# Masking every attention unit in one VectorE step instead of by way of GpSimd, with two small scalars of the first tiles moved to ScalarE

## The chip, the cores and the metric

The kernel runs on one core of one Trainium2 chip. The metric is the device time of one execution in microseconds, taken as the median of several executions. A profile is of one execution; its span is the time between the first and the last recorded instruction.

## The reference

Three layers follow one another on 1152 tokens (2 batches of 576) of width 512:

```python
# attention: B, H, S, D = 2, 8, 576, 64, all f32
scores = scale * np.matmul(q, k.transpose(0, 1, 3, 2))
kth = np.partition(scores, -32, axis=-1)[..., -32:-31]
scores = np.where(scores >= kth, scores, -1e9)
attn = np.exp(scores - scores.max(-1, keepdims=True))
attn = attn / (attn.sum(-1, keepdims=True) + 1e-9)
x = attn @ v                      # heads side by side: 1152 x 512
# mixture of 8 experts, all experts on all tokens, gates by 8 Sinkhorn rounds
for e in range(8):
    out += P[:, e:e+1] * (np.maximum(x @ w1[e], 0) @ w2[e])   # 512 -> 1024 -> 512
# a last feed-forward layer, 512 -> 2048 -> 512, with Mish between the products
```

So each row of attention keeps only the scores that reach its 32nd largest one.

## The kernel before, in words

The 1152 tokens are 9 tiles of 128 rows. A unit of attention is one tile t and one head h, 72 units in all, in the order of t and then h. Each unit passes five stages: `scores` (TensorE products, copied by ScalarE to a tile `s` of 128x576), `threshold` (VectorE takes the largest 8 values four times with `max`, and strikes them out three times with `match_replace`, which gives the 32 largest, `top`), `mask`, `norm` and `values` (TensorE turns the probabilities, multiplies by v, and the result becomes `xh` and `xl`, two float32r parts of x).

The first 13 units (`POOL_UNITS`) are "pooled". Their `mask` has three steps: VectorE writes 0 or a very negative number to `em` (L285), GpSimd adds the scores to it (L286), and ScalarE takes the exponential in place and sums it while it does so (L272, with VectorE writing the bias `nb`, the negated and scaled maximum, on L271). The other units take the exponential of all the scores to a tile `e` already in `threshold`, and `mask` is a single VectorE instruction, which compares, multiplies and sums (L290). In `norm`, VectorE adds epsilon to the sum (L299) and takes the reciprocal (L300), and ScalarE scales the unit's row (L305). Pooled units take `norm` and `values` one step later than the others.

Tiles 0 and 1 are the first chunk. Once their x is there, the experts' feed-forward passes of chunk 0 begin on TensorE (`h_c0e` on L619, `y_c0e` on L596), then those of chunk 1, with the rest of attention woven in between at a fixed rate; after attention, chunk 2 (`c2e`) and the last layer (`d`) follow. The first `max` of each unit of tile 2 is ordered on VectorE behind the last reciprocal of tile 1 (`live["ends"]`).

The order on TensorE is written out by hand: the plan runs step by step, and step i holds the scores of unit i, then the later stages of earlier units, then `early` scores of later tiles, which are kept in buffers of theirs or sent to memory. The orders on the other engines come from a planner, which takes the ready instruction of the highest priority: stream "first" is ahead of "evict", "prep" (weights, L517 to L522, with GpSimd computing the low parts `wl`), "attn" and "moe". Within a stream the order of the program counts. GpSimd also computes the low parts of k (`ks`, L158) and q (L188).

Rotating buffers: `top`, `nb`, `sm` and `r` have 4 each, `s` 6, `w` and `e` 2, and `em` 3 pairs.

Of the kernel before, what the change touches and what calls it, by code (L numbers as in the profile page):

```python
# [10 lines left out]
F32 = mybir.dt.float32  # L11
F32R = mybir.dt.float32r
U32 = mybir.dt.uint32
AF = mybir.ActivationFunctionType
ALU = mybir.AluOpType
# [4 lines left out]
P = 128  # L20
B, H, S, D = 2, 8, 576, 64
# [13 lines left out]
TOPK = 32  # L35
NEG = -3.0e38
SCALE = 0.125
EPS = 1e-9
TINY2 = ((1 + 1 / 16) * 2.0**-15) ** 2

CHUNKS = [(0, 1), (2, 3), (4, 5, 6, 7, 8)]
# [2 lines left out]
LAG = 2  # L44
LAG2 = 2
AHEAD = 2
POOL_UNITS = 13
EARLY = [(t, h) for t in (2, 3) for h in range(H)] + [(t, h) for t in (5, 6) for h in range(HG)]
EARLY_FROM, EARLY_PER_STEP = 5, 2
HOLD, RATE = 8, 0.25  # L50
# [23 lines left out]
def attention_moe_moe2(ctx: ExitStack, tc: tile.TileContext, qT, kT, vm, vt, wg, wst, w64, out):  # L74
    nc = tc.nc
    st = Streams(
        tc, {"first": 0, "evict": 200_000, "prep": 500_000, "attn": 1_000_000, "moe": 2_000_000, "fill": 3_000_000}
    )
    ctx.enter_context(tc.manual_schedule(engines={mybir.EngineType.PE}))

    def after(inst, earlier):

        tc.add_manual_dep(
            inst.ins,
            earlier.ins.name,
            mybir.DependencyInfo(mybir.DependencyClass.NoSync, mybir.DependencyReason.DATA),
            reason="order",
        )

    def pool(name, bufs=1, space=None, stack=ctx, side="left", **kw):  # L90
        if space is not None:
            kw["space"] = space
        return stack.enter_context(tc.tile_pool(name=name, bufs=bufs, side=side, **kw))

    const = pool("const")
    small = pool("small", 4)
# [13 lines left out]
    sp = pool("sp", 2, stack=att)  # L110
# [35 lines left out]
    qset, live, away = {}, {}, {}  # L146
# [45 lines left out]
    def queries(t, g):  # L192
        if (t, g) not in qset:
            qset[t, g] = load_q(t, g)
        return qset[t, g]
# [46 lines left out]
                load_v(t // 4, h // 2)  # L242
        yield

    def threshold(t, h, on_pool):

        with st("attn"):
            s = live["s", t, h]
            top = small.tile([P, TOPK], F32, tag="top", name=f"top_{t}_{h}")
            w = sp.tile([P, S], F32, tag="w", name=f"w_{t}_{h}")  # L250
            src = s
            for i in range(TOPK // 8):
                g = top[:, 8 * i : 8 * i + 8]
                top8 = nc.vector.max(g, src)  # L254
                if i == 0 and t == CHUNKS[0][-1] + 1:
                    if "ends" in live:
                        after(top8, live["ends"])
                    else:
                        live.setdefault("held", []).append(top8)
                if i + 1 < TOPK // 8:  # L260
                    nc.vector.match_replace(w, g, src, NEG)  # L261
                    src = w
            live["top", t, h] = top
            if not on_pool:
                live["e", t, h] = exponential(t, h, sp.tile([P, S], F32, tag="e", name=f"e_{t}_{h}"), s, nc.vector)
        yield from ()

    def exponential(t, h, dst, src, eng, **kw):

        nb = small.tile([P, 1], F32, tag="nb", name=f"nb_{t}_{h}")  # L270
        eng.tensor_scalar(nb, live["top", t, h][:, 0:1], -SCALE, None, op0=ALU.mult)  # L271
        nc.scalar.activation(dst, src, AF.Exp, bias=nb, scale=SCALE, **kw)  # L272
        return dst

    def mask(t, h, on_pool):

        with st("attn"):
            s = live.pop(("s", t, h))
            sm = small.tile([P, 1], F32, tag="sm", name=f"sm_{t}_{h}")
            kth = live["top", t, h][:, TOPK - 1 : TOPK]  # L280
            if h % 2 == 0:
                live["pair", t, h] = sp.tile([P, 2 * S], F32, tag="em", name=f"em_{t}_{h}", bufs=3)
            em = live["pair", t, h - h % 2][:, h % 2 * S :][:, :S]
            if on_pool:
                nc.vector.tensor_scalar(em, s, kth, NEG, op0=ALU.is_lt, op1=ALU.mult)  # L285
                nc.gpsimd.tensor_tensor(em, em, s, ALU.add)  # L286
                exponential(t, h, em, em, nc.vector, accum_out=sm)
            else:
                e = live.pop(("e", t, h))
                nc.vector.scalar_tensor_tensor(em, s, kth, e, op0=ALU.is_ge, op1=ALU.mult, accum_out=sm)  # L290
            live["em", t, h], live["sm", t, h] = em, sm
        yield from ()

    def norm(t, h, on_pool):
        with st("attn"):
            em, sm = live["em", t, h], live.pop(("sm", t, h))
            r = small.tile([P, 1], F32, tag="r", name=f"r_{t}_{h}")
            with st("moe" if on_pool else "attn"):
                nc.vector.tensor_scalar(r, sm, EPS, None, op0=ALU.add)  # L299
                inv = nc.vector.reciprocal(r, r)  # L300
            if (t, h) == (CHUNKS[0][-1], H - 1):
                live["ends"] = inv
                for inst in live.pop("held", ()):
                    after(inst, inv)
            nc.scalar.activation(em, em, AF.Copy, scale=r)  # L305
        yield from ()
# [96 lines left out]
    def attention():  # L403
        with st("attn"):
            load_k(0, 0)
            queries(0, 0)
            load_k(0, 1)
            wgraw = const.tile([P, NC, E], F32, name="wgraw")
            nc.sync.dma_start(wgraw, wg)
            nc.gpsimd.tensor_copy(wgs[:, :, :E], wgraw)  # L410
            nc.gpsimd.tensor_sub(wgs[:, :, E : 2 * E], wgraw, wgs[:, :, :E])
        units = [(t, h) for t in range(NT) for h in range(H)]
        plan = {}
        for u, (t, h) in enumerate(units):
            pooled = u < POOL_UNITS
            for order, (stage, delay) in enumerate(
                (
                    (scores, 0),
                    (partial(threshold, on_pool=pooled), AHEAD),
                    (partial(mask, on_pool=pooled), AHEAD + 1),  # L420
                    (partial(norm, on_pool=pooled), AHEAD + (2 if pooled else 1)),
                    (values, AHEAD + (3 if pooled else 2)),
                )
            ):
                plan.setdefault(u + delay, []).append((order, u, partial(stage, t, h)))
        stores = {}

        def early(t, h):

            k = EARLY.index((t, h))  # L430
            if k < 2:
                x = xfirst.tile([P, S], F32, tag=("xh1", "xl1")[k], name=f"early{k}")
            elif k < 10:
                name = ("xh2", "xl2")[(k - 2) // 4]
                if (k - 2) % 4 == 0:
                    stores[name] = xlast.tile([P, 4, S], F32, tag=name, name=f"early_{name}")
                x = stores[name][:, (k - 2) % 4, :]
            else:
                with st("attn"):
                    x = sp.tile([P, S], F32, tag="away", name=f"early{k}", bufs=2)  # L440
            yield from scores(t, h, x)
            if k >= 10:
                with st("attn"):
                    away[t, h] = dram.tile([P, S], F32, tag=f"away_{t}_{h}", name=f"away_{t}_{h}")
                    nc.sync.dma_start(away[t, h], live.pop(("s", t, h)))

        def fetch(t, h):
            with st("attn"):
                for b in range(t * P // S, (t * P + P - 1) // S + 1):
                    for i in range(h, h + HG):  # L450
                        if (b, i) not in ks:
                            load_k(b, i)
                queries(t, h // HG)
            yield from ()

        for k, (t, h) in enumerate(EARLY):
            step = EARLY_FROM + k // EARLY_PER_STEP
            plan[step].append((9, k, partial(early, t, h)))
            if h % HG == 0:
                plan[step - 2].append((8, k, partial(fetch, t, h)))  # L460
        for i in sorted(plan):
            runs = [run for _, _, run in sorted(plan[i], key=lambda x: x[:2])]
            blocks = 2 if i % 2 else 4
            for k, _ in enumerate(chain.from_iterable(run() for run in runs)):
                yield i + min(k + 1, blocks) / blocks
# [198 lines left out]


    at = attention()
    for _ in at:
        if live.get("done") == CHUNKS[0][-1]:
# [191 lines left out]
```

## Time and profile before

| | us |
|---|---|
| Time, median of 3 runs | 1221.68 (1221.15 to 1223.91) |
| Time of the profiled execution | 1221.39 |
| Span of the profile | 1219.6 |
| Busy PE / DVE / ACT / POOL in the span | 1168.7 / 854.7 / 660.2 / 540.8 |

PE is TensorE, PEld its weight loads, DVE is VectorE, ACT ScalarE, POOL GpSimd, SP the queue that issues most DMAs. Busy time counts the stretches in which an engine executes; a mean over the whole span hides that stages have different limits, so the stages have to be looked at one by one. Consecutive instructions of an engine overlap a little in the records, so what one costs its queue is the distance from its start to the next start.

### The profile page before, as it was taken

Reading aid. Unit: us, or ns where it says so; the run is one execution under the profiler, and the core shown is the slowest. Engines: PE = TensorE matmul, PEld = TensorE weight load, DVE = VectorE, ACT = ScalarE, POOL = GpSimd, SP = SyncE. Lnnn points to the kernel's source line nnn. Section 1 sums busy time; section 2 is a strip of 40 time slices with the busy share of each in tenths; the row PEclk is TensorE's granted clock in tenths of the full one; section 3 lists DMA queues with packets and bytes.
Section 4 is the critical chain, followed back from the end, with each engine's and each line's share of the span. In section 5 each row is a group of like instructions: output and inputs, shape, how many; then the busy total and the mean of one; then the engine's idle time right before and its main releaser. Section 6 shows DMA issues by size and latency. Waiting matters only on the chain.

```text
span 1219.6 us, 21194 instructions
## 1 busy us (share of the span) xinstructions
PE 1168.7 (96%) x7459; PEld 1048.4 (86%) x7459; DVE 854.7 (70%) x1873; ACT 660.2 (54%) x1321; POOL 540.8 (44%) x424
## 2 busy tenths in 40 slices
PE   2677999999999999999999999999999999999998
PEld 2566888998989899899999999999999999999997
DVE  7999999999999999713656868677666633433221
ACT  6786777877777778654223333333333334554432
POOL 7844778877777877774112112121121122221210
PEclk9899999999999999999999999999999999999999
DMA  8434565576655555665235665656445332223201
GB/s 258 126 129 152 171 178 170 170 224 188 211 163 168 157 162 164 186 220 169 70 89 180 199 190 176 207 178 192 138 134 160 119 98 64 93 95 114 78 26 44
DMA packets 105114, 183.20 MB, mean 150 GB/s; under 512 B 14128, under 2 KB 24624, under 8 KB 105008
## 3 DMA queue, kind: packets, MB, share of 16 engines
q1 hardware_dynamic: 103712, 180.68, 47.6%
q8 instruction: 58, 0.95, 0.3%
q10 hardware_dynamic: 1296, 1.18, 0.3%
q14 instruction: 48, 0.39, 0.1%
HBM read 158.55 MB, written 23.27 MB: 149 GB/s over the span
## 4 chain that ended last, share of the span: by engine, by line
PE 86%; DVE 11%; DMA 1%; ACT 1%; issue 0%; POOL 0%; SPq 0%; POOLq 0%; ACTq 0%
PE h_c2e L619 18%; PE y_c2e L596 18%; PE h_d L619 8%; PE y_d L596 8%; PE y_c0e L596 7%; PE h_c0e L619 7%; PE h_c1e L619 6%; PE y_c1e L596 6%; DVE top L254 4%; DVE w L261 4%; PE pv L348 2%; PE tr L325 2%; PE sc L226 2%; PE pv L355 1%; DVE em L290 1%; DMA wraw_c0e<-in_wst_dram 1%
## 5 line engine op out<-in xcount | busy, mean ns | idle before, releaser
L522 POOL TENSOR_TENSOR wl_c2e<-wraw_c2e,wh_c2e 128x512 fp32r<-128x512 f32 x64 | 84.2, 1315 | 341.2 <-ACT wh_c2e L520 326.5
L522 POOL TENSOR_TENSOR wl_c0e<-wraw_c0e,wh_c0e 128x512 fp32r<-128x512 f32 x128 | 171.6, 1356 | 53.1 <-ACT wh_c0e L520 50.9
L522 POOL TENSOR_TENSOR wl_c1e<-wraw_c1e,wh_c1e 128x512 fp32r<-128x512 f32 x128 | 173.3, 1371 | 48.6 <-ACT wh_c1e L520 45.2
L520 ACT ACTIVATE wh_c2e<-wraw_c2e 128x512 fp32r<-128x512 f32 x128 | 80.8, 632 | 186.9 <-PE y_c2e L596 95.0
L254 DVE MAX8 top<-w 128x8 f32<-128x576 f32 x216 | 157.8, 747 | 0.8
L619 PE MATMUL h_c2e<-xh,wh_c2e 128*128 128x256 f32 (+1 forms) x512 | 158.3, 309 | 0.0
L619 PE MATMUL h_c2e<-xl,wh_c2e 128*128 128x256 f32 (+1 forms) x512 | 158.0, 309 | 0.0
L619 PE MATMUL h_c2e<-xh,wl_c2e 128*128 128x256 f32 (+1 forms) x512 | 157.8, 308 | 0.0
L538 DVE SCALAR_TENSOR_TENSOR hl_c2e<-h_c2e,hh_c2e 128x256 fp32r<-128x256 f32 (+1 forms) x128 | 62.5, 488 | 99.7 <-ACT hh_c2e L537 99.3
L596 PE MATMUL y_c2e<-wh_c2e,hh_c2e 128*128 128x512 f32 x320 | 126.0, 394 | 0.0
L596 PE MATMUL y_c2e<-wl_c2e,hh_c2e 128*128 128x512 f32 x320 | 125.9, 394 | 0.0
L596 PE MATMUL y_c2e<-wh_c2e,hl_c2e 128*128 128x512 f32 x320 | 125.2, 391 | 0.0
L522 POOL TENSOR_TENSOR wl_d<-wraw_d,wh_d 128x512 fp32r<-128x512 f32 x32 | 41.5, 1297 | 160.2 <-ACT wh_d L520 160.2
L520 ACT ACTIVATE wh_c0e<-wraw_c0e 128x512 fp32r<-128x512 f32 x128 | 80.5, 629 | 52.9 <-PE y_c0e L596 21.0
L261 DVE MATCH_REPLACE8 w<-top,w 128x576 f32<-128x576 f32 x144 | 106.4, 740 | 0.0
L557 DVE TENSOR_TENSOR hl_d<-mg_d,hh_d 128x256 fp32r<-128x256 f32 x64 | 38.5, 602 | 91.7 <-ACT hh_d L556 91.7
L520 ACT ACTIVATE wh_c1e<-wraw_c1e 128x512 fp32r<-128x512 f32 x128 | 80.3, 629 | 40.4 <-PE y_c1e L596 16.4
L619 PEld LDWEIGHTS h_c2e<-xh,wh_c2e 128*128 128x128 f32 x512 | 96.2, 188 | 2.5
L619 PEld LDWEIGHTS h_c2e<-xl,wh_c2e 128*128 128x128 f32 x512 | 96.1, 188 | 2.3
L619 PEld LDWEIGHTS h_c2e<-xh,wl_c2e 128*128 128x128 f32 x512 | 96.8, 189 | 0.0
L226 PE MATMUL sc<-ks,q 128*128 128x288 f32 x320 | 63.1, 330 | 26.0 <-ACT early L239 8.2
L537 ACT ACTIVATE hh_c2e<-h_c2e 128x256 fp32r<-128x256 f32 (+1 forms) x128 | 54.8, 428 | 55.3 <-PE h_c2e L619 53.0
(170 smaller groups left out, 3352.8 us busy)
## 6 DMA issues: line engine op xcount, KB each, us to landing
wraw_c0e<-in_wst_dram SPq DMA_DIRECT2D x128, 256.0 KB, 3.0
wraw_c1e<-in_wst_dram SPq DMA_DIRECT2D x128, 256.0 KB, 3.0
wraw_c2e<-in_wst_dram SPq DMA_DIRECT2D x128, 256.0 KB, 3.0
cx<-in_w_dram SPq DMA_DIRECT2D x32, 512.0 KB, 4.2
wraw_d<-w SPq DMA_DIRECT2D x64, 256.0 KB, 2.6
yd<-ysp SPq DMA_DIRECT2D x32, 256.0 KB, 3.6
yb<-yd SPq DMA_DIRECT2D x32, 256.0 KB, 3.2
w<-cc SPq DMA_DIRECT2D x32, 256.0 KB, 3.5
```

The costliest lines, as they stand in the source:

```text
L226: nc.tensor.matmul(halves[half], q[:, h % HG, :], ks[b, h][:, half * HS : (half + 1) * HS], start=(i == 0), stop=(i == len(terms) - 1),)
L254: top8 = nc.vector.max(g, src)
L261: nc.vector.match_replace(w, g, src, NEG)
L325: nc.tensor.transpose(tr[:, c, :], em[:, j * D + c * P :][:, :P], ident)
L348: nc.tensor.matmul(pv[i * D : (i + 1) * D, pair, c0:c1], vmain[b, pair][:, i, c, :], live["at", i][:, c, c0:c1], start=(c == 0), stop=False,)
L520: nc.scalar.activation(hi, raw, AF.Copy)
L522: eng.tensor_sub(lo, raw, hi)
L537: nc.scalar.activation(h, ps, AF.Relu)
L538: live["hl"] = nc.vector.scalar_tensor_tensor(l, ps, 0.0, h, op0=ALU.max, op1=ALU.subtract)
L557: nc.vector.tensor_sub(l, g, h)
L596: nc.tensor.matmul(y, h[:, j * P : (j + 1) * P], w, start=(f == 0 and k == 0), stop=(f == nf - 1 and k == 2),)
L619: nc.tensor.matmul(ps, w[:, c * P : (c + 1) * P], x[:, c, c0 : c0 + m], start=(k == 0), stop=(k == 3 * NC - 1),)
```

## The change

All 72 units now take the path that before only the units behind the 13th took: the exponential of all the scores is taken in `threshold`, and one VectorE instruction masks and sums. The GpSimd addition, the three-step mask and the pooled units' extra step ahead of `norm` and `values` are gone. For tiles 0 and 1, the bias `nb` and the sum with epsilon are computed by ScalarE copies (with a scale, and with a bias) instead of by VectorE; for the later tiles they stay on VectorE. `norm` has the priority of attention throughout. `top`, `nb` and `sm` get 6 buffers.

```diff
-POOL_UNITS = 13
...
-    def threshold(t, h, on_pool):
+    def threshold(t, h):
...
-            top = small.tile([P, TOPK], F32, tag="top", name=f"top_{t}_{h}")
+            top = small.tile([P, TOPK], F32, tag="top", name=f"top_{t}_{h}", bufs=6)
...
-            if not on_pool:
-                live["e", t, h] = exponential(t, h, sp.tile([P, S], F32, tag="e", name=f"e_{t}_{h}"), s, nc.vector)
+            live["e", t, h] = exponential(t, h, sp.tile([P, S], F32, tag="e", name=f"e_{t}_{h}"), s)
...
-        nb = small.tile([P, 1], F32, tag="nb", name=f"nb_{t}_{h}")
-        eng.tensor_scalar(nb, live["top", t, h][:, 0:1], -SCALE, None, op0=ALU.mult)
-        nc.scalar.activation(dst, src, AF.Exp, bias=nb, scale=SCALE, **kw)
+        nb = small.tile([P, 1], F32, tag="nb", name=f"nb_{t}_{h}", bufs=6)
+        top = live["top", t, h][:, 0:1]
+        if t <= CHUNKS[0][-1]:
+            nc.scalar.activation(nb, top, AF.Copy, scale=-SCALE)
+        else:
+            nc.vector.tensor_scalar(nb, top, -SCALE, None, op0=ALU.mult)
+        nc.scalar.activation(dst, src, AF.Exp, bias=nb, scale=SCALE)
...
-            sm = small.tile([P, 1], F32, tag="sm", name=f"sm_{t}_{h}")
+            sm = small.tile([P, 1], F32, tag="sm", name=f"sm_{t}_{h}", bufs=6)
...
-            if on_pool:
-                nc.vector.tensor_scalar(em, s, kth, NEG, op0=ALU.is_lt, op1=ALU.mult)
-                nc.gpsimd.tensor_tensor(em, em, s, ALU.add)
-                exponential(t, h, em, em, nc.vector, accum_out=sm)
-            else:
-                e = live.pop(("e", t, h))
-                nc.vector.scalar_tensor_tensor(em, s, kth, e, op0=ALU.is_ge, op1=ALU.mult, accum_out=sm)
+            e = live.pop(("e", t, h))
+            nc.vector.scalar_tensor_tensor(em, s, kth, e, op0=ALU.is_ge, op1=ALU.mult, accum_out=sm)
...
-            with st("moe" if on_pool else "attn"):
+            if t <= CHUNKS[0][-1]:
+                nc.scalar.activation(r, sm, AF.Copy, bias=EPS)
+            else:
                 nc.vector.tensor_scalar(r, sm, EPS, None, op0=ALU.add)
-                inv = nc.vector.reciprocal(r, r)
+            inv = nc.vector.reciprocal(r, r)
...
-                    (partial(threshold, on_pool=pooled), AHEAD),
-                    (partial(mask, on_pool=pooled), AHEAD + 1),
-                    (partial(norm, on_pool=pooled), AHEAD + (2 if pooled else 1)),
-                    (values, AHEAD + (3 if pooled else 2)),
+                    (threshold, AHEAD),
+                    (mask, AHEAD + 1),
+                    (norm, AHEAD + 1),
+                    (values, AHEAD + 2),
```

## Rows read from the trace of the kernel before

**Rows 1.** Stretches: us, busy time of each engine (instructions), PE clock, DMA share, GB/s.

```profile
0.00:17.00 17.00, 5.53 (x16) 3.97 (x16) 9.99 (x23) 9.43 (x18) 11.49 (x24) 1.00 0.78 233
17.00:55.00 38.00, 18.91 (x86) 14.85 (x88) 36.29 (x82) 27.58 (x57) 34.05 (x25) 0.93 0.66 201
55.00:104.50 49.50, 37.09 (x255) 29.66 (x251) 49.43 (x131) 42.28 (x100) 20.98 (x18) 0.91 0.42 138
104.50:122.30 17.80, 14.31 (x102) 12.24 (x102) 17.80 (x43) 10.78 (x22) 8.91 (x7) 1.00 0.35 105
122.30:512.00 389.70, 389.29 (x2899) 348.82 (x2899) 380.40 (x931) 295.85 (x576) 306.89 (x230) 1.00 0.58 178
557.00:1219.60 662.60, 658.58 (x3797) 598.61 (x3795) 351.16 (x648) 247.80 (x499) 121.82 (x94) 1.00 0.40 127
```

**Rows 2.** Chain that ended last, 104 to 123 us: start, duration, what.

```profile
104.47 0.16 DVE r L300
104.63 2.63 DVE top L254 x4
...
121.89 0.33 DVE hl_c0e L538
122.23 0.04 issue
122.27 0.74 PE h_c0e L619 x4
```

**Rows 3.** Groups by shape on VectorE, 7 to 104.5 us: busy, mean ns | idle before.

```profile
L285 DVE TENSOR_SCALAR em<-s,top 128x576 f32<-128x576 f32 x13 | 10.9, 842 | 0.0
L290 DVE SCALAR_TENSOR_TENSOR em<-s,top,e 128x576 f32<-128x576 f32 x3 | 2.4, 811 | 0.0
L299 DVE TENSOR_SCALAR r<-sm 128x1 f32<-128x1 f32 x16 | 2.2, 140 | 0.0
```

**Rows 4.** VectorE in order of time: start, duration, instruction, idle before and releaser.

```profile
25.62 0.15 DVE L271 TENSOR_SCALAR nb<-top 128x1 f32<-128x1 f32 x1 [0.85 <-ACT em L272]
25.69 0.14 DVE L299 TENSOR_SCALAR r<-sm 128x1 f32<-128x1 f32 x1
25.75 0.80 DVE L285 TENSOR_SCALAR em<-s,top 128x576 f32<-128x576 f32 x1
...
55.39 0.50 DVE L285 TENSOR_SCALAR em<-s,top 128x576 f32<-128x576 f32 x1
55.81 0.75 DVE L254 MAX8 top<-w 128x8 f32<-128x576 f32 x1
...
103.28 0.82 DVE L290 SCALAR_TENSOR_TENSOR em<-s,top,e 128x576 f32<-128x576 f32 x1
104.03 0.08 DVE L290 DVE_READ_ACCUMULATOR em<-s,top,e 128x1 f32 x1
104.08 0.29 DVE L363 TENSOR_TENSOR xl<-pv,xh 128x128 fp32r<-128x128 f32 x1
104.29 0.14 DVE L299 TENSOR_SCALAR r<-sm 128x1 f32<-128x1 f32 x1
104.47 0.16 DVE L300 RECIPROCAL r<-r 128x1 f32<-128x1 f32 x1
```

**Rows 5.** Waits of VectorE, 17 to 105 us: total us, times, longest.

```profile
DVE nb L271 <- ACT em L272: 1.2, 2, 0.8
```

**Rows 6.** One line, L290, 200 to 500 us: durations in ns, min/median/max.

```profile
L290 DVE SCALAR_TENSOR_TENSOR em<-s,top,e x42: 800/1010/1891, 199.8 to 493.6; 128x576 f32<-128x576 f32 x42
```

**Rows 7.** Groups by shape on VectorE, 200 to 500 us.

```profile
L290 DVE SCALAR_TENSOR_TENSOR em<-s,top,e 128x576 f32<-128x576 f32 x42 | 47.8, 1141 | 0.5
```

**Rows 8.** Stretch 200 to 500 us, all engines (columns as in rows 1).

```profile
200.00:500.00 300.00, 299.59 (x2245) 268.96 (x2244) 293.33 (x709) 229.84 (x448) 236.27 (x177) 1.00 0.59 179
```

**Rows 9.** GpSimd instructions of L286 alone, by stretch: us, busy (instructions), clock, DMA.

```profile
17.00:55.00 38.00, 8.70 (x6) 0.93 0.66 201
55.00:104.50 49.50, 9.90 (x7) 0.91 0.42 138
```

**Rows 10.** Groups by shape on GpSimd, 17 to 104.5 us.

```profile
L286 POOL TENSOR_TENSOR em<-em,s 128x576 f32<-128x576 f32 x13 | 18.6, 1431 | 10.5 <-DVE em L285 8.2 <-DVE r L299 2.3
L158 POOL TENSOR_TENSOR ks<-kraw,ks 64x576 fp32r<-64x576 f32 x7 | 10.0, 1422 | 1.0 <-ACT ks L157 0.7
```

**Rows 11.** ScalarE in order of time: the table warm-up, and an accumulator read.

```profile
2.02 0.20 ACT L118 ACTIVATE warm<-warm 128x1 f32<-128x1 f32 x1
...
25.40 0.19 ACT L272 ACTIVATION_READ_ACCUMULATOR em<-em,nb 128x1 f32 x1
25.49 0.61 ACT L520 ACTIVATE wh_c0e<-wraw_c0e 128x512 fp32r<-128x512 f32 x1
```

**Rows 12.** Waits of ScalarE, 17 to 105 us: total us, times, longest.

```profile
ACT em L305 <- DVE r L300: 3.1, 5, 1.1
ACT wh_c0e L520 <- DMA wraw_c0e<-in_wst_dram: 2.3, 3, 1.5
```

More of the change, by code (lines that the diff above doesn't have):

```diff
@@ L263, in threshold, with exponential, mask @@
             live["top", t, h] = top
-            if not on_pool:
-                live["e", t, h] = exponential(t, h, sp.tile([P, S], F32, tag="e", name=f"e_{t}_{h}"), s, nc.vector)
+            live["e", t, h] = exponential(t, h, sp.tile([P, S], F32, tag="e", name=f"e_{t}_{h}"), s)
         yield from ()
-    def exponential(t, h, dst, src, eng, **kw):
-        nb = small.tile([P, 1], F32, tag="nb", name=f"nb_{t}_{h}")
-        eng.tensor_scalar(nb, live["top", t, h][:, 0:1], -SCALE, None, op0=ALU.mult)
-        nc.scalar.activation(dst, src, AF.Exp, bias=nb, scale=SCALE, **kw)
+    def exponential(t, h, dst, src):
+        nb = small.tile([P, 1], F32, tag="nb", name=f"nb_{t}_{h}", bufs=6)
[5 more added lines that the diff above has]
+        nc.scalar.activation(dst, src, AF.Exp, bias=nb, scale=SCALE)
         return dst
-    def mask(t, h, on_pool):
+    def mask(t, h):
         with st("attn"):
             s = live.pop(("s", t, h))
-            sm = small.tile([P, 1], F32, tag="sm", name=f"sm_{t}_{h}")
+            sm = small.tile([P, 1], F32, tag="sm", name=f"sm_{t}_{h}", bufs=6)
             kth = live["top", t, h][:, TOPK - 1 : TOPK]
@@ L283, in mask, with norm @@
             em = live["pair", t, h - h % 2][:, h % 2 * S :][:, :S]
-            if on_pool:
-                nc.vector.tensor_scalar(em, s, kth, NEG, op0=ALU.is_lt, op1=ALU.mult)
-                nc.gpsimd.tensor_tensor(em, em, s, ALU.add)
-                exponential(t, h, em, em, nc.vector, accum_out=sm)
-            else:
-                e = live.pop(("e", t, h))
-                nc.vector.scalar_tensor_tensor(em, s, kth, e, op0=ALU.is_ge, op1=ALU.mult, accum_out=sm)
+            e = live.pop(("e", t, h))
+            nc.vector.scalar_tensor_tensor(em, s, kth, e, op0=ALU.is_ge, op1=ALU.mult, accum_out=sm)
             live["em", t, h], live["sm", t, h] = em, sm
         yield from ()
-    def norm(t, h, on_pool):
+    def norm(t, h):
         with st("attn"):
@@ L414, in attention @@
         for u, (t, h) in enumerate(units):
-            pooled = u < POOL_UNITS
             for order, (stage, delay) in enumerate(
```

## The prediction

> **What bounds the kernel now.** I read the busy times by stretch first, because the change touches only the first 13 to 16 of 72 units. From 122.3 us on, TensorE is busy practically all the time: 389.29 of 389.70 us up to 512, 658.58 of 662.60 us behind 557 [rows 1]. Ahead of it, VectorE is what is full: 36.29 of 38 us, then 49.43 of 49.50, then 17.80 of 17.80 [rows 1]. The chain that ended last says the same: it runs on VectorE until 122.2 us and goes over to TensorE with a product of chunk 0 [rows 2]. So the time is some 122 us that VectorE sets, and behind them a TensorE schedule that neither the diff nor its loads alter. A microsecond taken from VectorE ahead of the last reciprocal of tile 1 (104.47 us) brings all that follows forward by about one, since tile 2's first `max` is ordered behind that reciprocal. GpSimd and ScalarE count only where VectorE waits for them.
>
> The sum is made against the profiled execution, 1221.39 us (span 1219.6, 1.8 around it), 0.3 under the median of 1221.68.
>
> **What goes from VectorE's queue.** Costs here are distances from start to start. (a) 13 two-operand masks L285: mean 842 ns [rows 3], of which about 0.08 overlaps the next instruction (0.50 recorded, next start after 0.42 [rows 4]): 13 x 0.76 = 9.9 us. (b) 16 biases `nb`: 25.62 to 25.69, 0.07 each, 1.1 us. (c) 16 sums with epsilon: 25.69 to 25.75, 0.06 each, 1.0 us [rows 4]. They are recorded with 0.14 [rows 3], yet the queue moves on after half of it. (d) Two waits of `nb`, 1.2 us [rows 5]: a buffer of `nb` was held by an exponential that ScalarE had not done. With six buffers and no `nb` on VectorE this form of the wait is gone. Together 13.2 us.
>
> **What comes to it.** 13 instructions of the form L290. Undisturbed, one takes 0.75 to its accumulator read and 0.05 for that at most [rows 4]; the three of this stretch average 811 ns recorded [rows 3]. With the overlap I take 0.77: 10.0 us. So on paper the change gives back 3.2 us. Note where it does not come from: in itself the new mask is dearer than the old one undisturbed (0.75 against 0.42 [rows 4]), and it only breaks even because the old one is already stretched from 0.50 to 0.84 [rows 3, 4].
>
> That stretching is the first unknown. L290 reads two tiles, and where GpSimd is busy it too is stretched: from 200 to 500 us, 42 of them average 1141 ns [rows 7], with a minimum of 800 and a maximum of 1891 [rows 6], while GpSimd is busy 236.27 of 300 us, 79% [rows 8]. That is 0.33 above the 0.81 of an undisturbed one, or 0.42 for a GpSimd that were always busy. Without L286, GpSimd is busy (34.05 - 8.70) / 38 = 67% from 17 to 55 us and (20.98 - 9.90) / 49.5 = 22% from 55 to 104.5 [rows 1, 9]. Some 6 of the new masks fall in the first stretch and 10 (the three old ones among them) in the second: 6 x 0.67 x 0.42 + 10 x 0.22 x 0.42 = 2.6 us. The bounds: nothing, as for the three rows here; and the worst row, 1.08 above the undisturbed one, for each of the six, with 0.9 for the rest, 7.4 us. I take 2.6, as its rows are the same instruction beside the same kind of GpSimd work.
>
> A rule of the Trainium skill can be weighed against this (SBUF — State Buffer, section "SBUF: two separate sides"): VectorE and GpSimd share a pair of ports, and a VectorE instruction with two inputs in SBUF and a GpSimd instruction that reads SBUF shut each other out for the whole of an instruction. By that, a mask that meets a GpSimd operation of 1.42 us [rows 10] would wait half of it on average, 0.7 instead of 0.42: 6 x 0.67 x 0.7 + 10 x 0.22 x 0.7 = 4.4 us, and the time would be 1.8 us above my sum. The rows agree in kind (nothing or up to 1.08 more) and not quite in size, and GpSimd can lose the race as well; I keep the rows' figure.
>
> **What becomes of the waits.** The second unknown is ScalarE. Each unit of tiles 0 and 1 gets two copies of 128x1 there. The nearest rows are a 128x1 activation of 0.20 and an accumulator read that occupies 0.09 of its queue [rows 11]; 32 copies at 0.1 to 0.2 are 3 to 6 us, less 13 accumulator reads, 1.2 us. ScalarE has that room: it is busy 27.58 of 38 and 42.28 of 49.5 us [rows 1], and the second becomes about 90%. The cover is thin there, but the bias costs VectorE nothing: it needs only the first of four `max`, and three more and three `match_replace` of about the same 0.66 [rows 2] follow, so that it and the exponential are due some 4 us ahead of the mask.
>
> The sum with epsilon is different. The reciprocal on VectorE now waits for a copy on ScalarE that itself waits for the mask, a round trip where there was none; queued behind that reciprocal is the whole of VectorE's work. As long as the planner puts a `max` of the next unit between (four take 2.63, 0.66 each [rows 2]), the round trip of about 0.3 us is covered. Two places have no such cover. At the last unit of tile 1, everything of tile 2 is ordered behind the reciprocal: 103.28 to 104.47 becomes about 0.4 us longer (a copy of 0.20 [rows 11] and two handings over between engines, put at 0.1 each as an estimate: within VectorE the next dependent one starts 0.04 behind, 104.43 to 104.47 [rows 4]). And while ScalarE stands at a weight copy whose DMA has not landed (2.3 us in three waits [rows 12]), a reciprocal behind it stands too, much as `nb` did before: I put half of the old 1.2 us back, 0.6.
>
> **Moved without cost.** `norm` and `values` of 13 units come one step sooner. They issue no DMA there. On TensorE the scores of the next unit stand behind the turned probabilities, one step sooner, but the scores are needed on VectorE only two steps later, over 10 us of cover at 16 units in 104.5 us [rows 1]; if that cover were gone, `top` would wait for `s`. The 18.6 us of GpSimd [rows 10] are off the path and worth only the contention counted above. The extra buffers are of at most 128 bytes a row.
>
> **The sum.** -13.2 + 10.0 + 2.6 + 0.4 + 0.6 = +0.4 us: 1221.39 + 0.4 = 1221.8 us, no change that can be told. About 0.2%, 2.4 us, is what a measurement of this kernel can tell from no change.
>
> **Rivals.**
> *Faster: the new masks find GpSimd quiet.* Nothing is added for contention and the reciprocals are covered: -3.2 + 0.4 = -2.8, 1218.6 us; with the 0.4 covered as well 1218.2. For it: GpSimd loses a quarter to a half of its work in these stretches [rows 1, 9], and three of three late masks were undisturbed [rows 3]. Against it: 67% remains in the first stretch, as k, q and the prefetched weights are still split there. It decides when contention and waits stay under 0.8 us together.
> *Slower: ScalarE's queue stands in front of each reciprocal.* If the planner's idea of ScalarE is ahead of the chip, each of 15 reciprocals waits for half of the ScalarE instruction in front (0.61 for a weight copy [rows 11], so 0.31): 4.6 in place of the 0.6, 0.4 + 4.0 = +4.4, 1225.8 us. For it: 90% busy, and ScalarE takes its instructions strictly in order. Against it: ScalarE today more often waits for VectorE's reciprocal (3.1 us) than the reverse [rows 5, 12], so it tends to be ahead. It decides from a mean wait of 0.17 us a reciprocal.
> *Slower: GpSimd's work falls on the masks.* With the upper bound of 7.4 in place of 2.6, +5.2, 1226.6 us. It decides when the masks of 17 to 55 us average over 1.4 us recorded.
>
> **Chances and range.** Forecast (within 0.2%) 0.45. Faster by over 0.2%: 0.28. Slower by over 0.2%: 0.27, of it 0.17 by ScalarE and 0.10 by GpSimd. The two signs are nearly even because the 3.2 us on paper and each unknown are of one size. The range goes from a little under the faster rival, 1217.3, to about the slower ones, 1226.5; the forecast's own is 1219.4 to 1224.2.
>
> **What would show it.** No L285 and L286; 16 masks on L290 ahead of the last reciprocal, averaging about 0.97 us recorded (undisturbed: 0.81; the GpSimd rival: over 1.2). No `nb` or epsilon on VectorE ahead of that reciprocal. The last reciprocal of tile 1 at 104.9 rather than 104.47 us; at 101.5 the faster rival is right. Waits of VectorE for `r` on ScalarE of about 1 us in all; 4 or more make the ScalarE rival right. TensorE full from 122 to 123 us and unchanged behind it. I am wrong altogether if the stretch behind 122 us changes its length: then the planner has ordered the later work differently, which no row of before can show.

## The result, and the profile after

The changed kernel takes 1233.72 us (median of 4 runs, 1233.41 to 1234.01), beside 1222.80 for the kernel before in the same runs (4 runs, 1221.15 to 1224.36): a ratio of 1.0089, 95% interval 1.0072 to 1.0107. It is 10.9 us slower, and the forecast of 1221.8, with a range up to 1226.5, is missed by a wide margin. The profiled execution took 1234.01 us, with a span of 1232.2.

The stretches of after, in the columns of [rows 1]. The last one is as long as that of before, within 0.6 us:

```profile
17.00:55.00 38.00, 19.70 (x101) 15.74 (x102) 35.78 (x78) 28.16 (x65) 26.12 (x19) 0.93 0.67 204
55.00:104.50 49.50, 35.72 (x234) 29.03 (x232) 48.81 (x113) 39.23 (x101) 11.38 (x11) 0.85 0.40 134
104.50:122.30 17.80, 14.01 (x91) 11.75 (x91) 17.06 (x43) 9.41 (x21) 6.08 (x5) 0.90 0.29 80
122.30:512.00 389.70, 387.09 (x2846) 344.59 (x2846) 383.03 (x920) 291.82 (x570) 299.24 (x227) 1.00 0.57 176
570.00:1232.00 662.00, 658.56 (x3779) 595.61 (x3777) 350.30 (x646) 245.93 (x495) 120.04 (x92) 1.00 0.40 125
```

Two things differ. In the first three rows VectorE fills its time less than before: it stands for 2.2, 0.7 and 0.7 us, where it stood for 1.7, 0.1 and 0 [rows 1]. And in the fourth TensorE is as busy as before at a full clock, yet it does fewer instructions: 2846 in 387.09 us, 136.0 ns each, where it did 2899 in 389.29, 134.3 ns each [rows 1]. The last row says the same more weakly: 174.3 ns for each of 3779, after 173.4 for each of 3797 [rows 1].

The page's line of busy time, before and then after, says it for the whole kernel:

```profile
PE 1168.7 (96%) x7459; PEld 1048.4 (86%) x7459; DVE 854.7 (70%) x1873; ACT 660.2 (54%) x1321; POOL 540.8 (44%) x424
```

```profile
PE 1178.7 (96%) x7459; PEld 1052.1 (85%) x7459; DVE 862.2 (70%) x1854; ACT 659.9 (54%) x1340; POOL 518.8 (42%) x411
```

The same 7459 products keep TensorE busy 10 us longer. Where this comes in is seen when one and the same TensorE instruction is looked up in both traces. The table gives its start in a trace, less its start in the trace of before (us, each counted from the start of its own span); the columns behind the first belong to the experiments below.

| Instruction (its time before) | after | e1_shift | s128 | f2_shift512 | e2_home |
|---|---|---|---|---|---|
| `h_c0e`, the 40th (116.2) | +3.4 | +0.1 | 0.0 | -1.0 | +3.1 |
| `y_c0e`, the 150th (197.2) | +4.2 | +0.9 | +0.8 | -1.0 | +3.1 |
| `y_c0e`, the last (342.5) | +6.3 | +2.3 | +2.3 | -1.0 | +3.1 |
| `y_c1e`, the last (561.6) | +9.7 | +5.6 | +4.2 | +1.0 | +4.2 |
| `h_c2e`, the 1200th (904.8) | +10.9 | +6.8 | +5.4 | -2.1 | +1.1 |
| `y_d`, the last (1215.2) | +13.0 | +8.8 | +7.5 | -2.1 | +1.1 |

So after loses some 3 us until chunk 0 has begun, and then goes on losing, a little in every stretch. The chain of the trace of before and of after beside each other, in the middle of chunk 2 (start, duration, what; the next start is the end of a piece):

```profile
934.09 3.45 PE y_c2e L596 x15
937.54 3.46 PE h_c2e L619 x24
941.00 3.44 PE y_c2e L596 x15
```

```profile
934.46 3.50 PE h_c2e L617 x24
937.96 3.50 PE y_c2e L594 x15
941.46 3.50 PE h_c2e L617 x24
```

Fifteen `y` products take 3.50 us in place of 3.44, each 233 ns in place of 229, with nothing waiting and the granted clock at 1.00 in both. Nothing in the diff touches these lines.

The early loss is VectorE's. The chain of after around the last reciprocal of tile 1 answers to [rows 2, 4]:

```profile
105.36 0.78 ACT em L304
106.14 0.16 ACT r L296
106.30 0.02 issue
106.33 0.17 DVE r L299
106.49 3.94 DVE top L253 x6
...
113.58 0.19 DVE xl L362
...
125.26 0.34 DVE hl_c0e L536
125.59 0.04 issue
125.64 1.45 PE h_c0e L617 x10
```

The reciprocal comes at 106.33, 1.9 us later than at 104.47 [rows 2]. Behind it stand six `max` where four stood [rows 2], so that `xl`, the low part of x, follows 7.3 us behind the reciprocal; in the trace of before it follows 5.8 behind:

```profile
110.28 0.19 DVE xl L363
```

From `xl` to the product of chunk 0 it is 12.0 us in both, and so the product is 3.4 us late. The waits of VectorE up to 125 us (total, times, longest):

```profile
DVE top L253 <- ACT s L234: 5.2, 4, 2.2
DVE xl L362 <- ACT xh L361: 0.6, 1, 0.6
DVE r L299 <- ACT r L296: 0.3, 1, 0.3
```

In the trace of before the scores were waited for like this:

```profile
DVE top L254 <- ACT s L235: 3.4, 3, 1.9
```

The waits of `nb` [rows 5] are gone. Those for the scores `s` have grown from 3.4 us to 5.2; the one of 2.2 us is new. The reciprocals wait 0.3 us. By the trace, the wait of 0.6 us for `xh` comes from TensorE's clock: it is at the lower of its two levels, 1.2 GHz, from 97.6 to 104.4 us (the granted clock of the stretch 100 to 105 us is 0.56, before 1.00), and 16 `pv` products take 2.51 us there, where 16 took 1.58 before. From 88 to 96 us, ahead of that, TensorE had been busy for 5.1 of 8 us at a granted clock of 1.00. In e2_home, below, with the same instructions, the clock from 100 to 105 us is 0.96, and there is no such wait.

### The profile page after: what moved, and what is told of

Read it like the earlier page. It is cut to its first block, busy times and chain, and to the rows that moved or that the text cites. A ratio compares the mean times of both kernels' runs of the same rounds, so it can differ in the third digit from the quotient of the medians.

```text
span 1232.2 us, 21164 instructions
## 1 busy us (share of the span) xinstructions
PE 1178.7 (96%) x7459; PEld 1052.1 (85%) x7459; DVE 862.2 (70%) x1854; ACT 659.9 (54%) x1340; POOL 518.8 (42%) x411
## 4 chain that ended last, share of the span: by engine, by line
PE 89%; ACT 3%; DVE 3%; DMA 3%; POOL 1%; issue 0%; SPq 0%; POOLq 0%; ACTq 0%
PE y_c2e L594 18%; PE h_c2e L617 18%; PE h_d L617 8%; PE y_d L594 8%; PE y_c1e L594 7%; PE h_c1e L617 7%; PE h_c0e L617 6%; PE y_c0e L594 6%; PE pv L347 3%; PE sc L225 3%; PE tr L324 2%; PE pv L354 1%; DVE top L253 1%; DVE w L260 1%; DMA away<-early 1%; DVE em L287 1%
## 5 line engine op out<-in xcount | busy, mean ns | idle before, releaser
L520 POOL TENSOR_TENSOR wl_c1e<-wraw_c1e,wh_c1e 128x512 fp32r<-128x512 f32 x128 | 169.7, 1342 | 57.0 <-ACT wh_c1e L518 56.4
```

The lines of the kernel that those rows point to most:

```text
L520: eng.tensor_sub(lo, raw, hi)
```

## The experiments

**The theories.** A: the buffers added to `top`, `nb` and `sm` push up all that lies behind them in the same memory, and TensorE's operands, in their new place, are read more slowly. Two more `top` of 128 bytes a row and two more each of `nb` and `sm`, which take 32 bytes, make 2 x 128 + 4 x 32 = 384 bytes. In the built kernels x, k, q, v, `s` and the hidden tiles `hh` and `hl` all lie 384 bytes a row higher in after; the weights lie where they did, but for the second ones of the last layer, which are moved as well. Of the two operands of a product one streams through the array, and the other is loaded into it first and stays (the weight loads of the trace, 128x128 each): in the `h` products x streams and the weights stay, in the `y` products the weights stream and the hidden tiles stay. B: another order of instructions slows TensorE. C: the pairs of PSUM banks, which after uses in exchanged order, matter. D, on the remainder: `values` one step sooner makes VectorE wait for scores.

**e1_shift: the kernel before, with 384 bytes that nothing uses.**

```diff
+    small.tile([P, 96], F32, tag="pad", name="pad", bufs=1)
```

> The kernel before, with an unused tile of 384 bytes a row placed in the pool of the small tiles: every tile behind it (x, the hidden parts, k, q, the scores, the accumulators) lies 384 bytes higher, exactly as in the changed kernel, while the weights' tiles on the other side and the order of instructions on every engine stay as before. Theory A (TensorE's pace depends on where its operands lie, and the changed kernel moved them with its extra buffers): about 7 us slower than before, some 1228.5, products y of chunk 2 at 3.50 us for 15 in place of 3.44, first product of chunk 0 where it was. Theory B (the slower pace comes from the changed order or from the banks of PSUM): no change, within 1 us of before.

Measured: 1229.7 us, ratio 1.0063 (1.0045 to 1.0081). The orders of all engines are those of before. Chunk 0 begins when it did, and from its 40th `h` to the last `y_d` the products fall behind by 8.8 us, in after by 9.6 (table above). The chain in the same part of chunk 2:

```profile
933.82 3.50 PE y_c2e L597 x15
937.32 3.50 PE h_c2e L620 x24
```

A tile that no instruction reads or writes costs 0.63%. B falls: no order has changed here.

**e2_home: the changed kernel, with TensorE's operands where they were.** The six-buffer tiles go to a place behind all other tiles of attention, and a filler keeps the rest in place.

```diff
+    far = pool("far", 6, stack=att)
+    small.tile([P, 192], F32, tag="pad", name="pad", bufs=1)
...
-            top = small.tile([P, TOPK], F32, tag="top", name=f"top_{t}_{h}", bufs=6)
+            top = far.tile([P, TOPK], F32, tag="top", name=f"top_{t}_{h}")
...
-        nb = small.tile([P, 1], F32, tag="nb", name=f"nb_{t}_{h}", bufs=6)
+        nb = far.tile([P, 1], F32, tag="nb", name=f"nb_{t}_{h}")
...
-            sm = small.tile([P, 1], F32, tag="sm", name=f"sm_{t}_{h}", bufs=6)
+            sm = far.tile([P, 1], F32, tag="sm", name=f"sm_{t}_{h}")
```

> The changed kernel with the same instructions in the same order and the same six buffers, but the tiles that have six buffers lie at the far end of the memory, and a filler of 768 bytes a row stands in their old place, so that TensorE's operands (but for the turned probabilities) lie where they lay in the kernel before. Theory A (addresses): 7 us of the 12 go, about 1226.5, with the later start of chunk 0 (some 3.4 us) and the pause of TensorE near 352 us (some 2.4) left. Theory B (order or banks): still about 1233.7.

Measured: 1223.55 us, ratio 1.0021 (1.0009 to 1.0034). The instructions and their order are those of after, and the pace is that of before:

```profile
938.65 3.45 PE h_c2e L619 x24
942.10 3.44 PE y_c2e L596 x15
```

With e1_shift this takes the loss apart: 1.0063 x 1.0021 = 1.0084, where the whole change measured 1.0089. About 7.7 us are addresses, about 2.6 us all else that the change does.

**e5_banks: the kernel before with the PSUM pairs exchanged.**

```diff
+    for i in range(2):
+        ps_m.tile([P, 512], F32, tag="mm2", name=f"first_{i}", bufs=2)
```

> The kernel before with the two pairs of PSUM banks of the feed-forward products exchanged, as they are in the changed kernel, by asking for the second pair first; nothing else differs, neither the order of instructions nor an address outside PSUM. Theory A (addresses in the other memory): within 1 us of before. Theory C (the banks set TensorE's pace): about 7 us slower, some 1228.5.

Measured: 1222.18 us, ratio 1.0003 (0.9987 to 1.0019). C falls.

**How far the move matters: f2_shift512, s128, s256.** The line of e1_shift with 128, 32 and 64 elements, so 512, 128 and 256 bytes.

> The kernel before with an unused tile of 512 bytes a row in place of the 384 of the run e1_shift; same orders, same weights. If what counts is where a tile begins within some power of two of up to 512 bytes: the time of before, 1220 to 1223. If any move away from the old places costs, or the distance to the weights on the other side: slower, 1226 to 1230.

> The same with 128 bytes: operands begin 256 bytes behind a multiple of 512. If only the multiple itself is slow: the time of before, 1219 to 1222. If the period is 256: as slow as the move of 384, about 1228.

> The kernel before with an unused tile of 256 bytes a row ahead of TensorE's operands: x and the hidden parts, which begin 128 bytes behind a multiple of 512 before, begin 384 behind one. The move of 384 put them on the multiple itself and cost 7.7 us; the move of 512 cost nothing. If only beginning on the multiple is slow: the time of before, 1219 to 1222. If the cost grows with the distance from the old place: 4 to 8 us slower.

Measured: a move of 512 bytes gives a ratio of 0.9999 (0.9990 to 1.0009), of 256 bytes 1.0003 (0.9988 to 1.0018), of 128 bytes 1.0050 (1.0037 to 1.0063). The chain of s128:

```profile
932.45 3.50 PE y_c2e L597 x15
935.94 3.50 PE h_c2e L620 x24
```

and that of f2_shift512:

```profile
935.48 3.46 PE h_c2e L620 x24
938.94 3.44 PE y_c2e L597 x15
```

So within these steps of 128 bytes the period is 256: moves of 0, 256 and 512 are quick, moves of 128 and 384 slow. Where only the multiple of 512 bytes was expected to be slow, that was wrong. In the built kernels x of chunk 2 begins at byte 27776 of its row before, 128 behind a multiple of 256, and at 28160 = 110 x 256 after: a start on the multiple is the slow one for the tiles moved here.

One layer does not follow. In the `y_d` products the streamed weights are moved together with the hidden tiles, and the mean distance from one start to the next (those under 260 ns, so without waits) is 229.2 ns in before, after and e1_shift alike, where `y_c2e` goes from 229.5 to 233.0. So it may be the places of a product's two operands relative to each other that count, and not the place of one by itself. No run tells these two apart.

**f3_round: the changed kernel with 128 bytes of filler,** which makes the whole move 512.

```diff
+    small.tile([P, 32], F32, tag="pad", name="pad", bufs=1)
```

> The changed kernel with an unused tile of 128 bytes a row behind its extra buffers, so that they move the operands by 512 bytes instead of 384; same orders as the changed kernel. If 512 is a whole period of what counts: 10 us of the loss go but for the later start, about 1223.5, as e2_home. If not: still about 1230 to 1234.

Measured: 1223.4 us, ratio 1.0024 (1.0015 to 1.0033). One line gives back what e2_home gives back with a rearrangement; from 1.0089 to 1.0024 it is some 8 us.

**Which operand it is: hid384 and x384.** In hid384 only the hidden tiles of chunks 0 and 1 are moved, by 384 bytes. In x384 x of chunks 0 and 1 is moved by 384, with k, q, v and `s`, and the hidden tiles by 512.

```diff
+    hp.tile([P, 96], F32, tag="pad2", name="pad2", bufs=1)
```

```diff
+    xfirst.tile([P, 96], F32, tag="pad", name="pad", bufs=1)
+    hp.tile([P, 32], F32, tag="pad2", name="pad2", bufs=1)
```

> The kernel before with 384 unused bytes a row ahead of the hidden parts hh and hl of chunks 0 and 1 alone: x, k, q, v, the scores, and all of chunk 2 and the last layer stay where they were. If the place of the operand that stays in the array (hh and hl, in the products y) sets the pace: six products y_c0e take 1.40 us in place of 1.37 and twelve h_c0e keep 1.39; the time is 2 to 3 us longer. If the moving operand does it (x, in the products h): no change.

> The counterpart: x of chunks 0 and 1, with k, q, v and the scores, lies 384 bytes higher, the hidden parts of those chunks 512, which as a move of its own cost nothing; chunk 2 and the last layer stay. If the moving operand sets the pace: twelve h_c0e take 1.41 to 1.42 us in place of 1.39, the six y_c0e keep 1.37, and the time is 2 to 3 us longer. If only the operand that stays counts: no change.

Measured: ratios of 0.9993 (0.9983 to 1.0003) and 0.9999 (0.9986 to 1.0012), so the 2 to 3 us that each was expected to cost did not show in the time. The traces show the pace, as the mean distance of the same kind:

| Mean distance, ns | before | after | hid384 | x384 |
|---|---|---|---|---|
| `y_c1e`, 512 columns | 230.2 | 233.6 | 232.5 | 230.4 |
| `h_c1e`, 256 columns | 119.7 | 121.6 | 119.6 | 121.5 |

So each kind follows the operand of its own that was moved: `h` the x that streams, `y` the hidden tiles that stay in the array, in hid384 by two thirds of the difference; the weights that `y` streams lie in the same place in all four. In chunk 0 the halves add up: from the 40th `h` to the last `y` hid384 loses 1.1 us against before and x384 1.3, e1_shift and s128 2.2 each, f2_shift512 0.1. The whole times do not show it: by the end of chunk 1 the trace of s128 is 4.1 us further behind than at its 40th `h`, and the two intervals allow 0.4 and 1.5 us at most. Why stays open.

**e3_masks: one-step masks alone.** The kernel before with no pooled unit: bias and epsilon on VectorE, four buffers, all addresses those of before.

```diff
-POOL_UNITS = 13
+POOL_UNITS = 0
```

> The kernel before with no pooled unit: all 72 units masked in one VectorE step, but bias and epsilon on VectorE, four buffers as before, so TensorE's operands lie where they lay. Theory A with the masks alone to blame for the later start: chunk 0 starts 3 us later, 1225 to 1227, pace of TensorE as before. Rival (the ScalarE copies make the later start): the start is within 1 us of before and the time within 1221 to 1223. By theory B it would be about 1230 or more, as the order of values and of the masks is the new one.

Measured: 1229.34 us, ratio 1.0075 (1.0054 to 1.0097), worse than expected, and worse than the whole change at these addresses (1.0021). The waits of VectorE up to 125 us:

```profile
DVE top L254 <- ACT s L235: 6.7, 5, 2.3
DVE xl L363 <- ACT xh L362: 1.7, 1, 1.7
```

The masks make VectorE wait for scores and for x, and the 40th `h` of chunk 0 begins 5.8 us later than before. The last `y_d` is 6.6 us late, so almost all of it is lost ahead of chunk 0, and TensorE's pace behind it is that of before. So something else in the change gives some 6 us back: the six buffers, or the scalars on ScalarE.

**f4_scalars: ScalarE's bias and epsilon alone,** with the pooled masks kept.

```diff
-        eng.tensor_scalar(nb, live["top", t, h][:, 0:1], -SCALE, None, op0=ALU.mult)
+        top = live["top", t, h][:, 0:1]
+        if t <= CHUNKS[0][-1]:
+            nc.scalar.activation(nb, top, AF.Copy, scale=-SCALE)
+        else:
+            eng.tensor_scalar(nb, top, -SCALE, None, op0=ALU.mult)
...
-                nc.vector.tensor_scalar(r, sm, EPS, None, op0=ALU.add)
+                if t <= CHUNKS[0][-1]:
+                    nc.scalar.activation(r, sm, AF.Copy, bias=EPS)
+                else:
+                    nc.vector.tensor_scalar(r, sm, EPS, None, op0=ALU.add)
```

> The kernel before with the ScalarE half of the change alone: bias and epsilon of tiles 0 and 1 come from ScalarE, the 13 pooled units stay pooled, no buffer is added, no address moves. By my prediction's terms VectorE's queue loses 2.1 us and may wait 1 us for ScalarE: 1 us faster than before, 1220. If ScalarE's queue stands in front of VectorE here: no change or up to 3 us slower, since pooled units need bias and sum late.

Measured: 1219.33 us, ratio 0.9992 (0.9980 to 1.0004): no change that can be told. VectorE's 32 small instructions are gone, but its reciprocals wait for ScalarE:

```profile
DVE r L307 <- ACT r L304: 3.4, 4, 1.8
```

**m4_scalars and e4b_home_vector: the two candidates apart.** The first is e3_masks with the diff of f4_scalars, so one-step masks, ScalarE's scalars and four buffers. The second is e2_home with bias and epsilon on VectorE, so one-step masks, VectorE's scalars and six buffers. TensorE's operands lie as before in both.

> The kernel before with all 72 units masked in one VectorE step and with bias and epsilon of tiles 0 and 1 on ScalarE, but four buffers for top, nb and sm, so that every operand of TensorE lies where it did before. Theory A: ScalarE's scalars are what makes the change at home addresses (ratio 1.0021) some 6 us better than the masks alone (1.0075); then this run is at about 1.002, and its masks wait little for nb. Theory B: it is the six buffers; then this run stays at about 1.0075 (1229 us) with waits of VectorE for s and xh of 4 us and more.

> The changed kernel with its six-buffer tiles in a place that leaves TensorE's operands at their addresses of before, and with bias and epsilon of tiles 0 and 1 back on VectorE. Theory A (ScalarE's scalars make the 6 us): as the masks alone, 1.0075. Theory B (the six buffers make them): about 1.002 plus the queue slots of 32 small VectorE instructions, 2.1 us by the rows of before, so 1.002 to 1.004.

| One-step masks, addresses of before | scalars on VectorE | scalars on ScalarE |
|---|---|---|
| four buffers | 1.0075 (1.0054 to 1.0097), e3_masks | 1.0030 (1.0013 to 1.0048), m4_scalars |
| six buffers | 1.0056 (1.0037 to 1.0074), e4b_home_vector | 1.0021 (1.0009 to 1.0034), e2_home |

The scalars make the difference, 0.35 to 0.45%; the buffers make none that these intervals can tell. With the pooled masks the same scalars made no difference that can be told (f4_scalars). The start of chunk 0 agrees: its 40th `h` product is 5.8 and 6.2 us late with VectorE's scalars, 2.3 and 3.1 with ScalarE's. Against e3_masks, the waits of m4_scalars:

```profile
DVE top L254 <- ACT s L235: 5.1, 4, 1.9
DVE r L307 <- ACT r L304: 0.3, 1, 0.3
```

The last reciprocal of tile 1 is 4.2 us earlier in m4_scalars (105.33 after 109.57): 2.1 us are the 32 instructions that leave VectorE's queue, 3.0 are waits that are gone (for `s` and `xh`, net of the new one for `r`), and some 0.8 are lost on longer masks and other instructions. About 1 us of the wait for `xh` is TensorE's clock again: 16 `pv` products take 2.61 us in e3_masks, at a granted clock of 0.66 from 104 to 109 us, and 1.58 in before. Why the scores are sooner was not tried by itself.

**f1_late: e2_home with `values` of the first 13 units one step later,** as the pooled units had it.

```diff
-                    (values, AHEAD + 2),
+                    (values, AHEAD + (3 if u < 13 else 2)),
```

> The changed kernel with its operands back at the addresses of before (as in the run e2_home), and the last stage, values, of the first 13 units one step later again, as before, so that on TensorE the scores of unit 5 stand ahead of the turned probabilities of unit 0 and not behind them. Theory D (the later start of chunk 0 comes from scores that are queued behind probabilities which ScalarE delivers late): VectorE's wait of 2.2 to 2.6 us for the scores near 28 us is gone and the time falls by about that from the 1223.55 of e2_home, to about 1221.2. Rival E (the new masks, stretched beside GpSimd, make the later start): the wait goes or stays, the time stays at 1223 to 1224.

Measured: 1223.23 us, ratio 1.0018 (1.0009 to 1.0026), as e2_home. The wait for scores fell, and another came:

```profile
DVE top L255 <- ACT s L236: 3.7, 5, 1.9
DVE r L301 <- ACT r L298: 3.2, 2, 1.9
```

Theory D has the wait right and its worth wrong. The reciprocals now wait 1.9 us at 30.4, for a copy that stands in ScalarE's queue behind weight and k copies for whose DMAs ScalarE had waited, and 1.3 us at 54.5, for one behind copies of early scores for which ScalarE had waited 2.4 us for TensorE. In this trace chunk 0 begins even later than in that of e2_home, 4.9 us after before's. What VectorE wants from ScalarE's queue is late by one name or by the other.

**No version tried can be told to be quicker than the kernel before.** f3_round is the repaired change, and it is still 0.24% slower; f4_scalars can't be told apart from before.

## Why the prediction was wrong

**The step that failed** is "The extra buffers are of at most 128 bytes a row", costed at nothing. Their size is right, 384 bytes in all; what they cost is that everything behind them starts elsewhere. That is 7.7 us of the 10.9 by e1_shift, and 6.1 for the move of 128 bytes in s128. With it falls the sentence that the 122 us are followed by "a TensorE schedule that neither the diff nor its loads alter". I had named a longer stretch behind 122 us as the case in which I would be "wrong altogether", but for another cause, a new order by the planner; e1_shift shows the same loss with every order unchanged. No row of before could show it, as all of them are taken at one place.

**The remainder, term by term.** At before's addresses the change costs 2.6 us, not the 0.4 of the sum.
- What goes: 13.2 us, and that was right. The waits of `nb` are gone, and no `nb` or epsilon stands ahead of the last reciprocal.
- What comes: 16 masks average 930 ns, where 970 were expected:

```profile
L287 DVE SCALAR_TENSOR_TENSOR em<-s,top,e 128x576 f32<-128x576 f32 x16 | 14.9, 930 | 0.0
```

- Contention is (930 - 811) x 16 = 1.9 us for all 16, where 2.6 was taken. The traces of the other kernels with these 16 masks give 1.4 (e3_masks, mean 897) to 3.4 us (f1_late, mean 1026), so one trace does not settle its size. GpSimd is busy 69% and 23% of the two stretches, as was worked out (67% and 22%). Single masks show where it falls: 0.80 us at 24.21, and 1.84 at 31.45. The Trainium skill (SBUF — State Buffer, section "SBUF: two separate sides") has the two engines shut each other out for whole instructions; the trace agrees in kind, and the 4.4 us that I estimated from it are more than any of these traces gives. The GpSimd rival (over 1.2 us a mask) is wrong.
- Epsilon on ScalarE: "the last reciprocal's round trip", 0.4 us, is 0.36 by the trace (105.97, when the mask's accumulator read starts, to 106.33), of which VectorE waits 0.27. That is the only wait for `r` among the waits above, so the 0.6 for waits behind weight copies did not come, and the ScalarE rival, with 4, is wrong. ScalarE is busy 39.23 of 49.5 us, 79% and not 90%. This part of the change is a gain that I took too low: e3_masks beside m4_scalars shows that without it the masks cost over twice as much.
- "Moved without cost" is the second step that does not hold. The scores' "over 10 us of cover" was a mean over 104.5 us, and at the start there is none. In after the turned probabilities of unit 0 stand ahead of the scores of unit 5 on TensorE, and they wait for ScalarE, which had stood for a weight copy until 24.10. The scores are copied at 28.01, and VectorE waits:

```profile
24.10 0.63 ACT L518 ACTIVATE wh_c0e<-wraw_c0e 128x512 fp32r<-128x512 f32 x1 [1.35 <-DMA wraw_c0e<-in_wst_dram]
25.54 1.12 PE L324 MATMUL tr<-ident,em 128*128 128x128 f32 x4 [7.15 <-ACT em L304]
26.31 1.31 PE L225 MATMUL sc<-ks,q 128*128 128x288 f32 x4
28.01 0.63 ACT L234 ACTIVATE s<-sc 128x576 f32<-128x576 f32 x1
```

```profile
25.74 0.74 DVE L260 MATCH_REPLACE8 w<-top,w 128x576 f32<-128x576 f32 x1
28.67 0.76 DVE L253 MAX8 top<-s 128x8 f32<-128x576 f32 x1 [2.20 <-ACT s L234]
```

  In place of "`top` would wait for `s`" as an aside it should have been a term: the waits for `s` are 1.8 us longer than before. What that is worth in time is not shown, as f1_late takes this wait away and gains nothing.
- Not foreseen: two more `max` and two more `nb` between the last reciprocal and `xl`, 1.4 us. I took the reciprocal to move "all that follows" by as much; the planner put other work between.

Adding VectorE's queue up to the last reciprocal: masks +1.6 us (13.7 for 16 now, 9.9 and 2.2 for 13 and 3 before), bias and epsilon -2.1, waits +1.5 (6.1 where 4.6 were), `max` and `match_replace` slower by 0.6 over 112 of them; that is 1.6 of the 1.9 us. With the 1.4 behind it, chunk 0 starts 3.4 us late in the trace of after, and 3.0 in that of e2_home, whose time is 2.6 us longer than before's. This account is read from the traces; of its terms only the masks, the scalars and the later `values` were tried by runs.

**What stays open.** The traces of kernels at the same addresses differ by about 3 us over the first part of chunk 2 (24 `h` products take 3.53 us in the trace of before until some 905 us, 3.46 in that of e2_home), and by 1.3 to 2.0 us at one place, at 347 us (e5_banks, hid384, x384) or from 488 to 509 (f2_shift512, s256). Both come in kernels whose order is before's, and I know no cause. The sums by traces are uncertain by this much; the ratios are taken over 4 to 12 executions.

## What to carry to other kernels

A buffer more is not free because it is small: it moves all that is placed behind it, and an operand of the bounding engine can land in a slower place. Where a change alters an allocation, look up where the bounding engine's operands begin before and after, or run the kernel before with an unused tile of the same size; that one run tells an address from an order. And a cover that is a mean over a stretch says nothing of its first units, where loads are still landing: look for the queue that will stand there, since taking away one wait on it gives the next one its place.

## What the runs showed of the hardware

In this kernel TensorE's pace depends on where the operands of a product begin in their rows. Of the moves tried, in steps of 128 bytes, those of 128 and 384 are slow, and those of 256 and 512 as quick as none (1.0003 and 0.9999). Both kinds of operand do it. Float32r products of 512 columns (`y`) start on average every 233.6 ns in place of 230.2 in chunk 1 when the tiles that stay in the array (`hh`, `hl`) are moved and the streamed weights are not; those of 256 columns (`h`) every 121.6 in place of 119.7 when the streamed x is moved. Those of 384 columns start every 173 ns in after and in hid384 alike, and the `y_d` products, where both operands are moved, keep 229.2. It is some 1.5% of an instruction, with the clock granted in full, and 0.50 to 0.63% of the time of this kernel. Which pair of PSUM banks a product writes made no difference (1.0003).
